# RWKV-7 state recurrence followed by a GELU MLP on one core: wide DRAM rows for the weights and for x, a planner with measured transfer times and one PSUM reader at a time, and MLP work spread over its chunk

## The chip, the cores and the metric

One core of one Trainium2 chip. The metric is the device time of one execution, in microseconds (us). The comparison of before and after rests on runs on the same chip.

## The reference

An attention-like recurrence for 4 batches, 8 heads, 768 steps and head dimension 40, and an MLP on its output:

```
for t in range(S):
    y[:, :, t] = einsum('bhd,bhde->bhe', rt, state)
    Sa = einsum('bhde,bhe->bhd', state, at)
    state = state * wt[:, :, None, :] - einsum('bhd,bhe->bhde', Sa, bt) + einsum('bhd,bhe->bhde', vt, kt)
x = y.transpose(0, 2, 1, 3).reshape(3072, 320)          # tokens x (heads * 40)
h = x @ w_in                                            # 320 -> 2048
out = (h / (1 + exp(-1.702 * h))) @ w_out               # 2048 -> 320
```

All inputs but the two weights are float32; the weights arrive as float64 and are taken as 64-bit integers.

## The kernel before

**Chunks and units.** The 768 steps are cut into 12 chunks `c` of 64 steps. A chunk has two units `i = 2c + p`, one for each pair of batches, so there are 24. In a unit the recurrence over 64 steps is solved as matrix work for 16 (batch, head) pairs: decays (`decay`: logarithm, running sums, exponentials), score matrices (`prep`: tiles `ps_NT`, `ps_A`, `ps_Av`, `ps_RV`), the triangular solve in six levels (`solve`: `ps_N`, then `ps_level`, each level in two halves, with the results `W` and `E` copied from PSUM by ScalarE and VectorE), then `ps_saT`, `ps_M` and the readout `ps_y`. The state goes from unit `i` to `i + 2` through `zraw`, `bz` and `zT`. All matmuls are float32 on 64x64 quarters of the array, four side by side; the profile has two records for each.

**From y to the MLP.** When `ps_y` of a unit is done, VectorE adds the state's part (`y`), GpSimd or VectorE multiplies by the decays (`x`, line 783), the SyncE queue (SP) writes `x` to DRAM (`part_with`, line 793, two DMAs, `x_dram`) and reads it back with channels on partitions (`get_back`, line 797, two DMAs, `xT`). When both units of a chunk are back, the MLP of that chunk may start.

**MLP.** `mlp(c)` has 40 `up` tasks (160 matmuls of 256 columns into `ps_up`), four GELUs on ScalarE (line 819, into `g`), and 2 x 8 `down` tasks (128 matmuls of 320 columns into `ps_down`), copies of the result to `ob` and its store.

**Weights.** `weight` brings a float64 tile of 512 columns, splits each number into sign and exponent and 52 bits of fraction on VectorE and ScalarE, joins them by matmuls with the identity (`ps_weight`), and scales the result into `w_in_sb` or `w_out_sb`. There are 10 tiles of each. A tile is used in the order of the first chunk's MLP.

**What sets the order.** Nothing is issued as written: every step is a task of `Plan` with a rank, the engines that can do it with an estimated duration on each, the tiles that it reads and writes, and a PSUM pair (two banks; there are four pairs). `Plan.order` walks through an estimated time: whenever an engine is free it takes the ready task of the lowest rank that it can do. Ranks are 10 for each unit and from 10000 up for the MLP, so that MLP tasks fill what the recurrence leaves free on TensorE. The result is the instruction order of each engine; on the chip each engine follows its own list in order and waits where a task isn't ready. All DMAs are on SP's queue. The planner also estimates when TensorE's code arrives, in blocks of 256 instructions (`FETCH`), and picks a task with longer matmuls where the code would run out (`AHEAD`). The estimates are in `Task` (`ns + 60.0` on VectorE and ScalarE), `DELAY` (from an engine's end to the next engine's start) and the line of `wire` (1500 ns and 280 bytes per ns for a DMA).

Of the kernel before, what the change touches and what calls it, by code (L numbers as in the profile page):

```python
# [49 lines left out]
class Task:  # L50
    def __init__(self, rank, engines, fn, pair, most, size):
        self.instr, self.sbuf = engines.pop("instr", 0), engines.pop("sbuf", False)
        self.rank, self.fn, self.pair, self.most, self.size = rank, fn, pair, most, size
        self.engines = {e: ns + 60.0 if e in ("DVE", "ACT") else 1.15 * ns if e == "POOL" else ns for e, ns in engines.items()}
        self.after, self.then = set(), []


class Plan:
# [5 lines left out]
    BLOCK, FETCH, AHEAD = 256, (3450.0, 4250.0, 5000.0), 300.0  # L64
    DELAY = {"PE": 330.0, "DVE": 130.0, "ACT": 130.0, "POOL": 150.0, "SP": 100.0}
    ISSUE = 60.0
# [28 lines left out]
    def order(self):  # L95
        for n, t in enumerate(self.tasks):
            t.n, t.left, t.ready = n, len(t.after), 0.0
            for o in t.after:
                o.then.append(t)
# [3 lines left out]
        coming = [(0.0, t.n) for t in self.tasks if not t.left]  # L103
        heapq.heapify(coming)
        able, now, wire, out, many = [], 0.0, 0.0, [], set()

# [11 lines left out]
        def fetch(at):  # L118
            return self.FETCH[(wire > at + 1000.0) + (wire > at + 10000.0)]
# [12 lines left out]
        def ahead(t):  # L132

            return (issued % self.BLOCK + t.instr) * fetch(now) / self.BLOCK - (now + t.engines["PE"] - begun)

        while coming or able:
# [12 lines left out]
            if not took:  # L149
                later = [x for x in (*free.values(), *pairs) if now < x < float("inf")]  # L150
# [17 lines left out]
            if t.pair is not None:  # L168
                if t.pair not in held:
# [9 lines left out]
            for o in t.then:  # L179
                o.ready = max(o.ready, end + (0.0 if o.engines.keys() == {e} else self.DELAY[e]))  # L180
                o.left -= 1
                if not o.left:
                    heapq.heappush(coming, (o.ready, o.n))
# [3 lines left out]
        return out  # L187


@with_exitstack  # L190
def rwkv7_gelu_quick(ctx: ExitStack, tc: tile.TileContext, time_d, v_d, w_d, wc_d, ak_d, b_d, rv_d, w_in, w_out, out):
# [6 lines left out]
    DFF = w_in.shape[1]  # L198
    NF = DFF // 128
# [4 lines left out]
    W_IN, W_OUT, PIECE = 2, 25, 512  # L204
# [113 lines left out]

    w_in_sb = single("w_in_sb", [128, NK, NM, 128])
# [6 lines left out]
    def weight(n, rank, key, dst, parts):  # L326

# [12 lines left out]

        def fetch(t):
# [40 lines left out]
        plan.add(rank, {"SP": 60.0 * len(parts)}, fetch, writes=T("wt"), size=128 * PIECE * 8, **here)  # L382
# [9 lines left out]
    def weights():  # L392
        blocks = w_in.rearrange("(k p) (m r f) -> k r p m f", p=64, r=2, f=128)
        for n, (m, k) in enumerate(product(range(0, NM, 4), range(NK))):
            weight(n, W_IN + 0.2 * n, ("w_in", (m // 4, k)), w_in_sb[:, k, m:m + 4].rearrange("p m f -> p (m f)"),
                   [(HALF[r], slice(0, PIECE), blocks[k, r][:, m:m + 4]) for r in BITS])
        for n in range(NF * DM // PIECE):
            parts, at = [], PIECE * n
            while at < PIECE * (n + 1):
                f, o = divmod(at, DM)  # L400
                size = min(DM - o, PIECE * (n + 1) - at)
                parts.append((slice(0, 128), slice(at - PIECE * n, at - PIECE * n + size), w_out[f * 128:(f + 1) * 128, o:o + size]))
                at += size
            weight(n + 10, W_OUT + 0.8 * n, ("w_out", n), w_out_sb[:, PIECE * n:PIECE * (n + 1)], parts)
# [10 lines left out]
    def load_w(i):  # L415
        for name, of, src, n in (("wc", wc_of, wc_d, 528), ("logw", logw_of, w_d, DM)):
            plan.add(10 * i - 30, {"SP": 60.0}, lambda t, of=of, src=src: nc.sync.dma_start(of(i), src[i]),
                     writes=[(name, i)], size=128 * n * 4)

    def load(i):  # L420
        for name, of, src, n in (("ak", ak_of, ak_d, 1024), ("time", time_of, time_d, 3 * DM), ("b", b_of, b_d, 512),
# [6 lines left out]
            plan.add(10 * i - 4, {"SP": 60.0 * len(rows)}, go, writes=[(name, i)] + ([("v", i)] if name == "RV" else []),  # L428
# [71 lines left out]
    xT_of = lambda c: buf("xT", c, [128, NK, 256])  # L500
# [4 lines left out]
    def prep(i):  # L505
# [12 lines left out]
        for n, (name, dst) in enumerate((("kh", kh_of), ("bh", bh_of))):  # L518
            plan.add(R + 4, {"POOL": 900.0, "DVE": 490.0, "sbuf": True}, lambda t, n=n, dst=dst: of(t.engine).tensor_mul(  # L519
# [56 lines left out]
    def solve(i):  # L576
# [207 lines left out]
        plan.add(R + 6, {"DVE": 1200.0, "POOL": 2000.0, "sbuf": True}, decayed, reads=T("y", "FT"), writes=T("x"))  # L784


        rows = lambda: drams[i].rearrange("(j e d) n -> e d j n", e=2, d=D)

        def part_with(t):
            if i not in drams:  # L790
                drams[i] = dram.tile([DM, 2 * C], FP32, tag=f"x{i}", name="x_dram")
            for e in BITS:
                nc.sync.dma_start(rows()[e], x_of()[64 * e:64 * e + D].rearrange("p j b t -> p j (b t)"))

        def get_back(t):
            for h in HALF:
                nc.sync.dma_start(xT_of(c)[h, :, 128 * p:128 * p + 128], drams[i].rearrange("(k q) n -> q k n", q=64))
        plan.add(-50, {"SP": 120.0}, part_with, reads=T("x"), writes=T("xd"), size=DM * 512)
        plan.add(-50, {"SP": 120.0}, get_back, reads=T("xd"), writes=[("xT", c), ("xs", (c, p))], size=2 * DM * 512)
# [6 lines left out]
    def mlp(c):  # L806
        R = 10000 + 100 * c

        def up(q, m, k):
            def go(t):  # L810
                ph, x = psum(t, "ps_up"), xT_of(c)[:, k]
# [11 lines left out]
        def down(p):  # L823
# [23 lines left out]
            plan.add(-100, {"SP": 120.0}, store, reads=[("ob", serial), ("out", serial)], size=128 * DM * 4)  # L847
# [28 lines left out]
    tasks = plan.order()  # L876
# [72 lines left out]
```

## Time and profile before

| | before |
|---|---|
| times of three runs, us | 878.48, 886.21, 884.02 (median 884.02) |
| the profiled execution's own time, us | 885.12 |
| its span, first to last instruction, us | 883.1 |
| busy in it, us: TensorE matmul, weight load, VectorE, ScalarE, GpSimd | 806.9, 629.5, 460.7, 382.3, 138.7 |
| mean granted TensorE clock | 0.979 |
| DMA: packets, MB, share of 16 engines | 58523, 82.61, 30.4% for the kernel's own queue |

The span runs from the first to the last instruction; about 2 us of the execution lie around it. Matmul and weight load overlap, and four matmuls run side by side, so the busy time of a group of matmuls is the time in which at least one of them ran. A busy TensorE can still be slowed: in the records matmuls have modelled ends.

### The profile page before, as it was taken

The page shows a single profiled execution, that of the slowest core. Times are in us where ns is not written, and L with a number is a line of the kernel's source. Part 1 is how long each engine was busy: PE and PEld are TensorE (multiplying, and loading weights), DVE is VectorE, ACT ScalarE, POOL GpSimd, SP SyncE. Part 2 cuts the span into 40 slices and gives each one's busy share as a digit, 9 for nine tenths or more (in the row PEclk, how much of TensorE's full clock was granted, in tenths as well). Part 3 has the DMA queues.
Part 4 walks back from the last instruction along what each step waited for, and adds up shares of the span by engine and source line. Part 5 has one row for each costly group of instructions (what it writes and reads, how often), then busy time and mean ns, then how long its engine had stood idle before and what let it go on. Part 6 is the DMA issues. An engine that isn't in the chain of part 4 may idle for free.

```text
span 883.1 us, 51576 instructions
## 1 busy us (share of the span) xinstructions
PE 806.9 (91%) x24272; PEld 629.5 (71%) x24272; DVE 460.7 (52%) x796; ACT 382.3 (43%) x678; POOL 138.7 (16%) x203
## 2 busy tenths in 40 slices
PE   3778899999989989889989989999979979999997
PEld 2445667888888877777777767877767767688764
DVE  6676873546545556445545554544555445354300
ACT  5547655335447346345444254533344333532210
POOL 2202130202202112202202102211021031010000
PEclk9989999999999999999999999999989989999999
DMA  9866551313322323322314232313142041020000
GB/s 265 252 172 184 170 148 41 119 40 109 112 81 75 110 71 88 105 75 87 104 40 125 89 92 75 115 41 112 49 129 82 21 126 56 23 75 26 19 25 16
DMA packets 58523, 82.61 MB, mean 94 GB/s; under 512 B 5672, under 2 KB 41512, under 8 KB 58312
## 3 DMA queue, kind: packets, MB, share of 16 engines
q1 hardware_dynamic: 58312, 79.32, 30.4%
q8 instruction: 190, 3.11, 1.5%
q14 instruction: 21, 0.17, 0.1%
HBM read 71.43 MB, written 7.86 MB: 90 GB/s over the span
## 4 chain that ended last, share of the span: by engine, by line
PE 77%; DMA 8%; ACT 6%; issue 4%; DVE 3%; SPq 2%; ACTq 0%
PE ps_up L236 23%; PE ps_down L236 21%; PE ps_level L236 15%; PE ps_weight L236 4%; PE ps_y L236 3%; DMA xT<-x_dram 3%; ACT W L698 3%; DMA x_dram<-x 3%; PE ps_N L236 2%; PE ps_M L236 1%; PE ps_Av L236 1%; PE ps_saT L236 1%; DVE E L693 1%; PE ps_rz L236 1%; PE ps_RV L236 1%
## 5 line engine op out<-in xcount | busy, mean ns | idle before, releaser
L236 PE MATMUL ps_up<-xT,w_in_sb 64*64 64x256 f32 x3840 | 277.6, 387 | 18.2 <-DMA xT<-x_dram 12.8
L236 PE MATMUL ps_down<-w_out_sb,g 64*64 64x320 f32 x3072 | 239.4, 431 | 0.7 <-issue 0.4
L236 PEld LDWEIGHTS ps_up<-xT,w_in_sb 64*64 64x64 f32 x3840 | 154.7, 137 | 53.9 <-issue 14.2
L698 ACT COPY W<-ps_level 128x672 f32<-128x672 f32 (+1 forms) x169 | 102.6, 617 | 191.7 <-PE ps_level L236 166.4
L236 PEld LDWEIGHTS ps_level<-W,E 64*64 64x64 f32 x5888 | 146.8, 137 | 41.9 <-DVE E L693 8.7
L236 PE MATMUL ps_level<-W,E 64*64 64x64 f32 (+2 forms) x5888 | 152.7, 235 | 8.9 <-DVE E L679 2.2
L236 PEld LDWEIGHTS ps_down<-w_out_sb,g 64*64 64x64 f32 x3072 | 122.1, 133 | 51.7 <-issue 2.2
L693 DVE TENSOR_TENSOR E<-twice,ps_level 128x512 f32<-128x512 f32 x120 | 81.5, 685 | 102.5 <-ACT W L698 75.6
L519 POOL TENSOR_TENSOR kh<-time,G 128x320 f32<-128x320 f32 x23 | 20.6, 897 | 503.1 <-issue 390.2
L236 PEld LDWEIGHTS ps_level<-W 64*64 64x64 f32 x2560 | 60.2, 133 | 23.6 <-issue 15.5
L819 ACT ACTIVATE g<-ps_up 128x1024 f32<-128x1024 f32 x48 | 49.2, 1024 | 62.7 <-PE ps_up L236 62.5
L236 PE MATMUL ps_level<-W 64*64 64x64 f32 (+2 forms) x2560 | 63.9, 234 | 9.4 <-issue 7.6
L236 PE MATMUL ps_weight<-wt,full 128*128 128x512 f32 x80 | 44.9, 692 | 6.6 <-ACT wt L369 3.4
L783 POOL TENSOR_TENSOR x<-y,FT 128x128 f32<-128x128 f32 x88 | 48.6, 582 | 0.5 <-ACT y L775 0.5
L677 DVE TENSOR_TENSOR W<-edge,ps_level 128x672 f32<-128x672 f32 x40 | 33.8, 848 | 19.1 <-PE ps_level L236 18.9
L511 POOL TENSOR_TENSOR ak<-ak,FT 128x512 f32<-128x512 f32 x21 | 27.5, 1309 | 55.3 <-ACT FT L474 33.6
L236 PE MATMUL ps_y<-RV,kh 64*64 64x104 f32 x768 | 36.1, 250 | 0.0
L236 PE MATMUL ps_y<-M,bh 64*64 64x104 f32 x768 | 35.7, 249 | 0.0
L843 ACT COPY ob<-ps_down 128x320 f32<-128x320 f32 x21 | 8.9, 425 | 60.8 <-PE ps_down L236 60.8
L845 DVE TENSOR_TENSOR ob<-ob,ps_down 128x320 f32<-128x320 f32 x24 | 11.6, 483 | 44.7 <-ACT ob L843 44.5
L236 PEld LDWEIGHTS ps_weight<-wt,full 128*128 128x128 f32 x80 | 15.2, 208 | 25.3 <-issue 16.5
L763 DVE TENSOR_TENSOR zraw<-ps_y,bz 128x320 f32<-128x320 f32 x20 | 9.8, 491 | 43.7 <-PE ps_y L236 43.7
(110 smaller groups left out, 1054.1 us busy)
## 6 DMA issues: line engine op xcount, KB each, us to landing
time<-in_time SPq DMA_DIRECT2D x24, 480.0 KB
RV<-in_v SPq DMA_DIRECT2D x24, 416.0 KB
xT<-x_dram SPq DMA_DIRECT2D x48, 160.0 KB
ak<-in_ak SPq DMA_DIRECT2D x44, 160.0 KB
rv<-in_rv SPq DMA_DIRECT2D x44, 160.0 KB
wc<-in_wc SPq DMA_DIRECT2D x24, 264.0 KB
wt<-in_w_in SPq DMA_DIRECT2D x20, 256.0 KB
logw<-in_w SPq DMA_DIRECT2D x24, 160.0 KB
```

Of the source, the lines that this page charges most:

```text
L236: nc.tensor.matmul(o, lhsT, rhs, start=start, stop=True, skip_group_check=True)
L511: plan.add(R, {"DVE": 690.0, "POOL": 1270.0, "sbuf": True}, lambda t: of(t.engine).tensor_mul(ahT(), ahT(), FT_of(i)), reads=T("ak", "FT") ...
L519: plan.add(R + 4, {"POOL": 900.0, "DVE": 490.0, "sbuf": True}, lambda t, n=n, dst=dst: of(t.engine).tensor_mul(dst(i)[:, :, :D], by_head(t ...
L677: plan.add(key, dve(672), lambda t: nc.vector.tensor_sub(W_of(s + 1)[:, :, b], edge[:, :, b], item(t)[:, :, :, :168]), reads=T("edge"), wr ...
L693: plan.add(key, dve(512), lambda t: nc.vector.tensor_sub(E_of(es + 1)[:, :, b].rearrange("p h j (n t) -> p h (j n) t", n=2), wide(twice).t ...
L698: plan.add(key, any2(4 * (168 - lo)), lambda t: copy(t.engine)(W_of(s + 1)[:, :, b, :, lo:], item(t)[:, :, :, lo:168]), writes=keeps, pair ...
L763: nc.vector.tensor_add(new, got, bz_of(i)[:, :, 64:].rearrange("p (u j) d -> p u j d", u=2))
L783: of(t.engine).tensor_mul(x[:, b ^ u, b], y_of()[:, at], FT_of(i)[:, at])
L819: plan.add(-45, act(1024), lambda t: nc.scalar.activation(g_of(c * NQ + q).rearrange("p m r n -> p r m n"), psum(t, "").rearrange("p r (m ...
L843: plan.add(-45, any2(320), lambda t: copy(t.engine)(ob_of(serial), psum(t, "")[:, 0, :DM]), writes=[("ob", serial)], pair=("down", serial))
L845: plan.add(-45, dve(320), lambda t: nc.vector.tensor_add(ob_of(serial), ob_of(serial), psum(t, "")[:, 1, :DM]), reads=[("ob", serial)], wr ...
```

## The change

- **Weights** come from DRAM in tiles that are laid out before the launch: one DMA of 128 rows of 4096 bytes for each tile, where there were two DMAs with rows of 1024 bytes (`w_in`) or two and three with 512 to 2560 bytes (`w_out`).
- **x** goes to DRAM in rows of 2048 bytes and comes back in rows of 2560, where both were 512. The channels of x get another order for that; the rows of `w_in` are put in the same order.
- **Planner.** The 60 ns on VectorE and ScalarE tasks are gone and hand-over delays are shorter; DMA issue costs are larger (350 for one DMA, 700 for two, where it was 60 and 120), a DMA takes 1200 ns and then 400 bytes per ns divided by 1.3; the code fetch takes 3550 ns and more when DMAs run beside it. A task that reads a PSUM pair on VectorE isn't placed while ScalarE reads that pair in the plan, and the other way round (`unread`).
- **Spread MLP.** `paced` makes the plan four times. After each, every MLP matmul task of a chunk gets a time before which the planner may not take it (`release`): the tasks are spread in proportion to their TensorE time from the moment the chunk's first one was ready to the moment the next chunk's was, 5 us earlier. The plan with the earliest estimated end is kept. A release is not in the program: it only moves the task's place in the order.

```diff
-        self.engines = {e: ns + 60.0 if e in ("DVE", "ACT") else 1.15 * ns if e == "POOL" else ns for e, ns in engines.items()}
+        self.engines = engines
...
-    BLOCK, FETCH, AHEAD = 256, (3450.0, 4250.0, 5000.0), 300.0
-    DELAY = {"PE": 330.0, "DVE": 130.0, "ACT": 130.0, "POOL": 150.0, "SP": 100.0}
+    BLOCK, FETCH, BESIDE, AHEAD = 256, 3550.0, 0.4, 300.0
+    DELAY = {"PE": 300.0, "DVE": 60.0, "ACT": 60.0, "POOL": 150.0, "SP": 800.0}
+    LATENCY, RATE, SPREAD = 1200.0, 400.0, 1.3
...
+        def unread(t, e):
+            return max((x + 60.0 for o, x in last.get(t.pair, {}).items() if o != e), default=0.0) if t.pair is not None and e != "PE" else 0.0
...
-                    took = next((t for t in able if e in t.engines and fits(t)), None)
+                    took = next((t for t in able if e in t.engines and fits(t) and unread(t, e) <= now), None)
...
-                wire = max(wire, now + 1500.0) + t.size / 280.0
-                end = wire
+                wire = max(wire, end + self.LATENCY)
+                running.append((wire, wire + self.SPREAD * t.size / self.RATE))
+                end = wire = running[-1][1]
...
+    def paced(self, groups, rounds, window, share):
+        best = None
+        for n in range(rounds):
+            out = self.order()
+            end = max(t.start + t.engines[t.engine] for t in out)
+            if best is None or end < best[0]:
+                best = end, [(t, {**vars(t)}) for t in out]
+            for g, then in zip(groups, groups[1:]):
+                whole, done, begin = sum(t.engines["PE"] for t in g), 0.0, g[0].ready
+                for t in g:
+                    new = begin + share * (then[0].ready - begin) * done / whole - window
+                    t.release = new if n == 0 else 0.5 * (t.release + new)
+                    done += t.engines["PE"]
...
-            for p, cols, part in parts:
-                to = raw()[p, cols]
-                nc.sync.dma_start(to.rearrange("p (m f) -> p m f", m=part.shape[1]) if len(part.shape) > 2 else to, part)
...
-        plan.add(rank, {"SP": 60.0 * len(parts)}, fetch, writes=T("wt"), size=128 * PIECE * 8, **here)
+        plan.add(rank, {"SP": 350.0}, lambda t: nc.sync.dma_start(raw(), src), writes=T("wt"), size=128 * PIECE * 8, **here)
...
-    xT_of = lambda c: buf("xT", c, [128, NK, 256])
+    xT_of = lambda c: buf("xT", c, [128, 2, NK, 128])
...
-        rows = lambda: drams[i].rearrange("(j e d) n -> e d j n", e=2, d=D)
+        rows = lambda: drams[i].rearrange("(e d j) n -> e d (j n)", e=2, d=D)
...
-                nc.sync.dma_start(rows()[e], x_of()[64 * e:64 * e + D].rearrange("p j b t -> p j (b t)"))
+                nc.sync.dma_start(rows()[e], x_of()[64 * e:64 * e + D].rearrange("p j b t -> p (j b t)"))
...
-                nc.sync.dma_start(xT_of(c)[h, :, 128 * p:128 * p + 128], drams[i].rearrange("(k q) n -> q k n", q=64))
-        plan.add(-50, {"SP": 120.0}, part_with, reads=T("x"), writes=T("xd"), size=DM * 512)
+                nc.sync.dma_start(xT_of(c)[h, p].rearrange("q k n -> q (k n)"), drams[i].rearrange("(q k) n -> q (k n)", q=64))
+        plan.add(-50, {"SP": 700.0}, part_with, reads=T("x"), writes=T("xd"), size=DM * 512)
...
-    tasks = plan.order()
+    tasks = plan.paced(list(paces.values()), ROUNDS, WINDOW, SHARE)
```

**What it moves.** Instruction counts on TensorE stay as they are; the order changes throughout. Three places follow, with the row numbers left out (`x8` are eight matmuls that follow each other).

TensorE in the program before, from the end of unit 17's readout (`ps_y`), the last piece of chunk 8 that its MLP waits for; between these rows and the first `ps_up` of chunk 8 stand 18 more `ps_level` rows and no row of the MLP:

```order
L236 MATMUL ps_y<-RV,kh_108 64x104 x4
L236 MATMUL ps_y<-M,bh_110 64x104 x4
L236 MATMUL ps_N<-bz_123,ak_117 64x104 x16
L236 MATMUL ps_zT<-ident,bz_123 64x40 x16
L236 MATMUL ps_A<-ak_118 64x64 x16
L236 MATMUL ps_cum<-logw,incl 64x160 x4
L236 MATMUL ps_level<-W 64x104 x4
L236 MATMUL ps_level<-W 64x64 x4
```

The same place now; one more row of eight `ps_down` matmuls stands among the rows that follow before the first `ps_up` of chunk 8:

```order
L270 MATMUL ps_y<-RV,kh_108 64x104 x4
L270 MATMUL ps_y<-M,bh_110 64x104 x4
L270 MATMUL ps_down<-w_out_sb,g 64x320 x8
L270 MATMUL ps_N<-bz_123,ak_117 64x104 x16
L270 MATMUL ps_down<-w_out_sb,g 64x320 x8
L270 MATMUL ps_RV<-rv_121 64x64 x16
L270 MATMUL ps_cum<-logw,incl 64x160 x4
L270 MATMUL ps_down<-w_out_sb,g 64x320 x8
L270 MATMUL ps_level<-W 64x104 x4
L270 MATMUL ps_level<-W 64x64 x4
```

Here 32 matmuls of chunk 7's MLP moved from ahead of the readout to behind it. Over chunks 2 to 10 the `ps_up` and `ps_down` matmuls between a chunk's last `ps_y` and its first `ps_up` number 16, 40, 48, 16, 0, 56, 0, 8 and 32 in the program before (216 together), and 24, 16, 48, 40, 32, 32, 32, 56 and 40 now (320). For chunk 11 they are 80 and 96.

SP's queue around the write and the return of `x` of unit 17, before:

```order
L427 DMA ak_117<-in_ak 40x1024 x2
L417 DMA logw<-in_w 128x320
L793 DMA x_dram<-x 40x4x128 x2
L427 DMA b_120<-in_b 40x512 x2
L797 DMA xT<-x_dram 64x5x128 x2
L417 DMA wc<-in_wc 128x528
```

And now:

```order
L448 DMA b_120<-in_b 40x512 x2
L438 DMA logw<-in_w 128x320
L814 DMA x_dram<-x 40x512 x2
L818 DMA xT<-x_dram 64x640 x2
L438 DMA wc<-in_wc 128x528
L863 DMA out<-ob 64x320 x2
```

The load of `b` moved ahead of the write, and nothing stands between write and return. For units 3, 5, 7 and 13 the store of a result (`out`) stands between the two now; before it was so for units 5, 11 and 23.

SP's queue at the start of the program, the first weight tiles, before:

```order
L427 DMA RV<-in_v 128x832
L344 DMA wt<-in_w_in 64x4x128 x8
L427 DMA ak_118<-in_ak 128x1024
L427 DMA time<-in_time 128x960
L427 DMA b_120<-in_b 128x512
```

And now:

```order
L448 DMA RV<-in_v 128x832
L411 DMA wt<-in_w_in 128x512 x4
L448 DMA ak_118<-in_ak 128x1024
L448 DMA time<-in_time 128x960
L448 DMA b_120<-in_b 128x512
```

The place is the same; eight DMAs became four. Of ScalarE's table loads, which stand where GELU follows an exponential or a logarithm or the other way round, the program has 48 before and 40 now.

More of the change, by code (lines that the diff above doesn't have):

```diff
@@ L118, in fetch @@
         def fetch(at):
-            return self.FETCH[(wire > at + 1000.0) + (wire > at + 10000.0)]
+            took = self.FETCH
+            for _ in range(3):
+                beside = sum(max(0.0, min(y, at + took) - max(x, at)) for x, y in running[-8:])
+                took = self.FETCH + self.BESIDE / self.SPREAD * beside
+            return took
+        def unread(t, e):
+            return max((x + 60.0 for o, x in last.get(t.pair, {}).items() if o != e), default=0.0) if t.pair is not None and e != "PE" else 0.0
         def fetched(t, start):
```

69 lines of the change are left out of this document (38 added, 31 removed).

## The prediction

> **What bounds the kernel now.** I read the chain that ended last first, then stretches of the span, then the places where TensorE's share falls. The page, and the windows of the span (columns: stretch, its length, busy us of matmul, weight load, VectorE, ScalarE, GpSimd with their counts, granted clock, DMA share, GB/s):
>
> ```profile
> PE 77%; DMA 8%; ACT 6%; issue 4%; DVE 3%; SPq 2%; ACTq 0%
> 0.00:40.00 40.00, 19.48 (x616) 14.73 (x618) 26.93 (x54) 22.31 (x44) 11.64 (x27) 1.00 0.93 271
> 40.00:66.00 26.00, 21.57 (x341) 11.14 (x337) 18.69 (x34) 11.86 (x26) 1.44 (x2) 0.80 0.61 166
> 66.00:120.00 54.00, 47.63 (x1444) 32.50 (x1437) 40.28 (x71) 38.09 (x74) 12.01 (x16) 1.00 0.56 171
> 120.00:240.00 120.00, 118.71 (x3624) 98.08 (x3619) 64.81 (x109) 51.28 (x88) 21.09 (x30) 1.00 0.31 91
> 240.00:840.00 600.00, 561.07 (x17671) 449.04 (x17666) 308.53 (x526) 253.37 (x445) 92.48 (x128) 0.98 0.26 78
> 840.00:883.00 43.00, 38.43 (x636) 24.01 (x628) 1.46 (x3) 5.37 (x7) 0.00 (x0) 1.00 0.07 16
> ```
>
> TensorE holds the end: 77% of the chain are matmuls. It idles in two places: the start (40 - 19.5 and 26 - 21.6, together 25 us of the first 66) and the middle (600 - 561.1 = 39 us from 240 to 840, and a mean clock of 0.98 there, 12 us more). The rest is work that the change doesn't take away, since no matmul is removed.
>
> The middle's idle time has a place. I took, for chunks 2 to 11, the window from the end of the chunk's last `ps_y` to its first `ps_up`; the first, the seventh and the sum of the ten:
>
> ```profile
> 233.00:245.00 12.00, 9.38 (x364) 8.47 (x357) 9.38 (x16) 7.75 (x17) 6.75 (x9) 1.00 0.61 193
> 639.00:650.70 11.70, 6.61 (x294) 6.01 (x284) 8.57 (x14) 6.36 (x14) 6.47 (x9) 1.00 0.67 207
> sum 119.20, PE 93.63 PEld 78.25 DVE 83.38 ACT 52.88 POOL 53.56; mean PE 9.36 PEld 7.82 DVE 8.34 ACT 5.29 POOL 5.36
> ```
>
> 119.2 - 93.6 = 25.6 us of the 39 fall into 20% of the time: each chunk's x takes some 11 to 13 us from `ps_y` to `ps_up`, and TensorE has too little else to do. The chain in the seventh of them (start, us, what):
>
> ```profile
> 641.12 2.11 issue
> ...
> 644.82 2.62 DMA x_dram<-x
> ...
> 648.20 3.95 DMA xT<-x_dram
> ```
>
> The write and the return of x bound it, 6.6 us without what goes ahead. Behind them the granted clock falls; of six 20 us stretches from 240 on that show it, the first, the fifth and the last:
>
> ```profile
> 240.00:260.00 20.00, 17.69 (x609) 15.47 (x601) 10.96 (x20) 11.51 (x24) 2.93 (x3) 0.91 0.29 87
> 640.00:660.00 20.00, 13.87 (x410) 11.89 (x406) 11.82 (x20) 8.30 (x17) 6.14 (x9) 0.83 0.46 144
> 720.00:740.00 20.00, 17.40 (x536) 14.09 (x540) 7.43 (x15) 8.07 (x13) 0.12 (x1) 0.84 0.20 59
> ```
>
> **The change part by part.** All against the profiled execution's own 885.1 us (span 883.1), 1.1 us over the median of the runs shown.
>
> **1. MLP work behind the readout.** The unit prices of MLP matmuls, where they run alone at the end (two records for each matmul):
>
> ```profile
> 843.93 8.63 PE ps_up L236 x160
> 863.35 15.12 PE ps_down L236 x224
> ```
>
> 15.12 / 224 = 67.5 ns a record, 135 ns a `ps_down` matmul; 108 ns a `ps_up`. By the order, chunks 2 to 11 have 296 MLP matmuls in these windows before and 416 now. The 120 more are, at 135 ns, 16.2 us of work that depends on nothing there. It comes from places where TensorE runs without a gap (118.7 of 120 us from 120 to 240), so little is lost there. The bounds are 0 and the whole 25.6. I take **-15**: chunk 11 already had enough, chunk 3 gets less than before (16 for 40), but chunks 6, 8 and 9, the emptiest (0, 0, 8), get 32, 32 and 56, 4.3 us or more each. What is late next there is the level chain, whose steps wait for copies on ScalarE and VectorE.
>
> The SP queue is the other side of this part: between write and return of the odd units from 3 on nothing stands in six, a load in one (unit 15) and a store in four (3, 5, 7, 13). A store waits for a `ps_down` that the spread puts behind `ps_y`; it stands there where the plan has it ready before the write of x lands, so I cost it at nothing and keep it for the range.
>
> **2. The clock.** The lowered stretches follow chunks 2, 5, 6, 7, 8 and 9, with 16, 16, 0, 56, 0 and 8 MLP matmuls in the window; chunks 3, 4, 10 and 11, with 40, 48, 32 and 80, have none. So five of five windows with 16 or fewer lose it, and one of five with more. Now only chunk 3 has 16, and chunk 2 has 24. Two or three of seven such losses stay: 12 us become 4, **-8**, between 0 and -12.
>
> **3. Wide rows.** Rates where one kind of row prevails: 6 to 16 us (rows of 2 KB and up, later 1 KB), 30 to 36 (`w_in`, rows of 1 KB), 834 to 844 (x and a store, mostly 512 bytes):
>
> ```profile
> 6.00:16.00 10.00, 4.27 (x136) 4.04 (x136) 7.40 (x12) 4.94 (x13) 2.85 (x2) 1.00 1.03 325
> 30.00:36.00 6.00, 4.72 (x124) 3.01 (x124) 3.88 (x7) 2.49 (x5) 0.42 (x1) 1.00 1.00 267
> 834.00:844.00 10.00, 10.00 (x156) 5.69 (x152) 1.39 (x5) 0.43 (x2) 0.00 (x0) 1.00 0.25 67
> ```
>
> Per full share: 316, 267 and 268 GB/s. The sizes:
>
> ```profile
> wt<-in_w_in SPq DMA_DIRECT2D x20, 256.0 KB
> xT<-x_dram SPq DMA_DIRECT2D x48, 160.0 KB
> x_dram<-x SPq DMA_DIRECT2D x48, 80.0 KB
> ```
>
> `w_in`'s ten tiles are 5.2 MB, 19.6 us at 267 and 16.6 at 316: 3 us of a queue that is 0.93 busy in the first 40 us, ahead of the loads of unit 1. The chain of the start waits for these:
>
> ```profile
> 19.49 2.38 issue
> ...
> 44.15 3.31 DMA wt<-in_w_in
> ...
> 61.38 4.21 DMA wt<-in_w_in
> ```
>
> and, from the first row, for code that comes late while the queue is full. Three waits of 2 to 4 us, each shorter by a fifth, and 3 us less in front: **-5** for the start, between +2 (one large DMA where two small ones let others in) and -12 (half of the 25 us idle). For x, 0.49 MB a unit (two writes, two returns) at 316 for 268 is 0.28 us. Issuing the two returns costs less, too; one such row beside one of a load with a whole row for each partition:
>
> ```profile
> 17.83 0.33 SPq L427 DMA_DIRECT2D b<-in_b  x1
> 837.61 1.29 SPq L797 DMA_DIRECT2D xT<-x_dram  x2
> ```
>
> 1.29 becomes 0.66 or so: 0.9 us of 11, in the windows that still wait, which is inside the -15.
>
> The Trainium skill, "DMA: Bandwidth & Descriptors", section Specifications, gives 512 bytes as the least transfer for line rate. By it the x and `w_in` rows were wide enough, and the row part would bring 0 of the -5. The rates above speak against it by a sixth; I keep the rows.
>
> **4. Code.** TensorE's code comes in blocks:
>
> ```profile
> q8 instruction: 190, 3.11, 1.5%
> 620.00:640.00 20.00, 19.96 (x719) 15.21 (x710) 10.47 (x19) 6.24 (x14) 0.59 (x2) 1.00 0.19 51
> 540.41 1.18 PE ps_level L236 x64
> ```
>
> 3.11 MB in 190 blocks are 16 KB each. In the densest stretch 719 matmuls and as many weight loads went by in 20 us; at 256 instructions a block that is one in 3.56 us. A block of `ps_level` alone streams in 128 x 1.18 / 64 = 2.4 us, a block of `ps_down` in 8.6. So runs of small matmuls outrun their code, and the 4% "issue" of the chain (35 us, half of it at the start) is its price. I cut TensorE's order into blocks of 128 records and added each kind at its streaming price: 51 blocks were under 3.4 us, 36 are now; lifting every short block to 3.56 us costs some 7 us less than before. I take **-6**, between -10 (blocks at 4 us) and +5 (other blocks meet the loads now).
>
> The Trainium skill, "Runtime: NRT & Kernel Launch", section Instruction fetch mechanics, says that the fetch is hidden, because the sequencer dispatches slower than code arrives. By it this part is 0. The 2.1 and 2.4 us waits above that only "issue" ends speak against it.
>
> **5. ScalarE and VectorE.** 48 table loads become 40:
>
> ```profile
> L819 ACT ACT_TABLE_LOAD x20 | 25.7, 1283 | 1.7 <-PE ps_up L236 1.4
> ```
>
> 8 x 1.28 = 10.3 us of an engine that is 43% busy; perhaps a sixth lies on the chain: **-2**, between 0 and -10. Twenty `edge` pieces go from VectorE to ScalarE, 0.24 to 0.34 us each: **+1**. That a pair has one reader at a time adds no wait on the chip: there VectorE's `E` waits for ScalarE's `W` of the same pair already,
>
> ```profile
> L693 DVE TENSOR_TENSOR E<-twice,ps_level 128x512 f32<-128x512 f32 x120 | 81.5, 685 | 102.5 <-ACT W L698 75.6 <-PE ps_level L236 25.8
> ```
>
> 75.6 us in all, so the plan only learns of it.
>
> **Sum:** -15 - 8 - 5 - 6 - 2 + 1 = -35; 885.1 - 35 = **850 us**.
>
> **The rivals.**
>
> A, everything lands: parts 1 and 2 reach 25 and 12, the start 10, code 8, tables 4: -59, 826 us. For it: the windows are the whole pattern of the middle. Against: chunks 2 and 3 have 24 and 16 matmuls only.
>
> B, code takes over: where the gaps close, the same instructions have to come faster, and "issue" replaces the wait for x. Parts 1 and 2 bring half (-11), part 4 nothing, the rest stays (-6): 868. For it: waits for code stand in the windows too (641.12). Against: a block in 4.3 us was the mean from 120 to 840 (42590 instructions, 166 blocks), 3.56 is possible.
>
> C, the order isn't what the chip runs: gaps move to other places of the chunk, since the estimates fit no better; only the start and the tables come: 878.
>
> D, slower: the plan gave every VectorE and ScalarE step 130 ns of slack (60 on its time, 70 on the hand-over), which is gone. TensorE takes its list in order; where a `ps_level` stands too early, all behind it wait. There are 24 x 6 x 2 = 288 level groups. If each waits 0.13 us more, that is 37 us, and the gain is gone; the old slack on both copies of a step (0.26) would cost 75, 925 us. It decides from 0.12 us a group. I price it at 0.16: 46 us, 896. Against it, a hand-over as it runs:
>
> ```profile
> 29.18 0.73 ACT W L698
> 29.91 0.04 issue
> 29.95 0.96 PE ps_level L236 x40
> ```
>
> 0.04 us from copy to matmul: the shorter estimate of 60 ns is the nearer one.
>
> **How the numbers follow.** Forecast 0.52 (838 to 862), A 0.16, B 0.13, C 0.11, D 0.08. The range leaves out D and the lower part of A: **825 to 881**. A measurement of this kernel tells about 1% from no change. Under 875: forecast, A, nearly all of B, 0.79; within 1%: C and a little of B, 0.12; above: D and a mishap like it, 0.09.
>
> **What would show it.** Part 1: in the ten windows TensorE idles 10 us, not 25.6, with `ps_down` between the levels. Part 2: a clock of 0.99 or more, two or three dips in the middle. Part 3: 267 GB/s in the first weights become over 300, and the readout of unit 0 ends some 5 us ahead of 66. Part 4: "issue" 3% of the chain. Part 5: 40 table loads. Wrong it would be if idle time shows up at `ps_level` behind ScalarE or VectorE (D), or as long waits of the return of x behind a store.

## The result and the profile after

The changed kernel took 855.7 us (median of four runs, 842.8 to 865.8) where before took 885.1: a ratio of 0.9575 (95% interval 0.9493 to 0.9656). The ratio counts only runs within 1.5% of the fastest run of their kernel, here those of 842.8 and 849.6 us; the medians alone give 0.967. In a second measurement ("The changed kernel once more", below) it was 0.9655 (0.9597 to 0.9712). The forecast was 850. The profiled execution took 842.8 us, the fastest of its four, against 885.1 for that of before: -42.3 us to explain, some 13 more than the medians differ by.

The stretches of the changed kernel (the third stretch, 66 to 120 us, is left out; the last ends at 800 us, just ahead of the last chunk's MLP):

```profile
0.00:40.00 40.00, 26.58 (x696) 19.60 (x696) 31.29 (x60) 25.68 (x52) 14.09 (x30) 1.00 0.84 299
40.00:66.00 26.00, 17.55 (x356) 10.36 (x356) 19.28 (x36) 12.37 (x23) 4.92 (x6) 0.87 0.52 168
120.00:240.00 120.00, 116.46 (x3654) 97.25 (x3656) 64.26 (x102) 56.00 (x96) 22.62 (x32) 1.00 0.31 92
240.00:800.00 560.00, 540.80 (x17568) 459.22 (x17561) 309.92 (x524) 233.03 (x416) 94.64 (x130) 1.00 0.28 83
```

The middle idles 19.2 us in 560 where it idled 39 in 600, and its clock is 1.00 where it was 0.98. In the first 66 us TensorE is busy 7 us longer and then 4 us less: 26.6 us of the first 40 for 19.5, then 17.6 of 26 for 21.6. The windows from a chunk's last `ps_y` to its first `ps_up`, first, seventh and sum:

```profile
229.90:240.90 11.00, 9.33 (x345) 8.53 (x338) 10.01 (x16) 3.76 (x9) 6.44 (x9) 1.00 0.54 155
612.90:624.70 11.80, 10.38 (x362) 8.61 (x358) 9.90 (x17) 5.94 (x13) 6.46 (x9) 1.00 0.63 189
sum 116.90, PE 105.29 PEld 91.16 DVE 86.85 ACT 48.61 POOL 56.66; mean PE 10.53 PEld 9.12 DVE 8.69 ACT 4.86 POOL 5.67
```

They are as long as before (116.9 us for 119.2), so x comes back no sooner; they are fuller: 11.6 us idle for 25.6. TensorE's own list of waits has the return of x, before and after, as

```profile
PE ps_up L236 <- DMA xT<-x_dram: 12.8, 9, 3.3
```

```profile
PE ps_up L270 <- DMA xT<-x_dram: 4.4, 5, 1.5
```

(us in total, times, the longest).

How much of a stretch isn't work can be estimated from the trace: each matmul is priced at the spacing that its kind keeps where it runs without a gap at full clock (the streaming prices below), and the sum is taken from the length of the stretch. By that the time from the first `ps_up` of chunk 1 to that of chunk 11 has 43.9 us over the work in it, where it had 83.4. Of these 39.5 us, 14.0 are idle time of the windows, 13.6 are clock (27.2 us at half speed before, none now), and 12 are the rest, of which 5 are idle time between the windows and 7 aren't taken apart. The start, up to the first `ps_up`, has 39.7 us over its work for 43.8. Chunk 0's MLP, between the two, has 1.6 us more. The end (from chunk 11's first `ps_up`) has the same length, 39.3 and 39.4 us.

### The profile page after: what moved, and what is told of

Same layout as the page of the kernel before. It is cut to its first block, busy times and chain, and to the rows that moved or that the text cites. A ratio compares the mean times of both kernels' runs of the same rounds, so it can differ in the third digit from the quotient of the medians.

```text
span 841.1 us, 51510 instructions
## 1 busy us (share of the span) xinstructions
PE 787.0 (94%) x24272; PEld 653.6 (78%) x24272; DVE 470.3 (56%) x804; ACT 367.8 (44%) x657; POOL 143.6 (17%) x208
## 5 line engine op out<-in xcount | busy, mean ns | idle before, releaser
L270 PE MATMUL ps_up<-xT,w_in_sb 64*64 64x256 f32 x3840 | 268.1, 378 | 5.7 <-DMA xT<-x_dram 4.4
L270 PE MATMUL ps_down<-w_out_sb,g 64*64 64x320 f32 x3072 | 244.4, 431 | 1.8 <-DVE ob L866 1.5
L270 PEld LDWEIGHTS ps_up<-xT,w_in_sb 64*64 64x64 f32 x3840 | 158.2, 134 | 27.0 <-issue 4.0
L719 ACT COPY W<-ps_level 128x672 f32<-128x672 f32 (+1 forms) x157 | 97.5, 623 | 175.8 <-PE ps_level L270 164.9
L270 PEld LDWEIGHTS ps_down<-w_out_sb,g 64*64 64x64 f32 x3072 | 138.4, 133 | 36.4 <-issue 2.9
L270 PE MATMUL ps_level<-W,E 64*64 64x64 f32 (+2 forms) x5888 | 149.9, 230 | 8.0 <-issue 3.0
L270 PEld LDWEIGHTS ps_level<-W 64*64 64x64 f32 x2560 | 64.4, 137 | 17.1 <-issue 6.6
L866 DVE TENSOR_TENSOR ob<-ob,ps_down 128x320 f32<-128x320 f32 x24 | 11.6, 485 | 48.6 <-ACT ob L864 48.1
L761 DVE TENSOR_TENSOR M<-ps_M,upper 128x512 f32<-128x512 f32 x24 | 16.5, 690 | 38.3 <-PE ps_M L270 38.3
L719 DVE COPY W<-ps_level 128x672 f32<-128x672 f32 (+1 forms) x43 | 32.0, 745 | 9.2 <-PE ps_level L270 9.1
L646 ACT ACTIVATE edge<-W 64x160 f32<-64x160 f32 x64 | 21.4, 334 | 33.5 <-DVE W L625 32.9
```

The source lines that it names most:

```text
L270: nc.tensor.matmul(o, lhsT, rhs, start=start, stop=True, skip_group_check=True)
L646: nc.scalar.mul(dst, src, -1.0)
L719: plan.add(key, any2(4 * (168 - lo)), lambda t: copy(t.engine)(W_of(s + 1)[:, :, b, :, lo:], item(t)[:, :, :, lo:168]), writes=keeps, pair ...
L761: plan.add(R + 4, dve(512), lambda t: nc.vector.tensor_tensor(M_of(i)[:, :, :64].rearrange("p (e j) t -> p e j t", e=2), psum(t, "")[:, :, ...
L866: plan.add(-45, dve(320), lambda t: nc.vector.tensor_add(ob_of(serial), ob_of(serial), psum(t, "")[:, 1, :DM]), reads=[("ob", serial)], wr ...
```

## The experiments

All ratios are to runs of the kernel before on the same chip, with the 95% interval; the times in us are medians of all runs. Runs of one kernel differ by 3 to 25 us and a profile is of one of them, not always one near the median (876.2 us for rows alone, 856.9 without the spread), so small differences between profiles are used only where several agree. "Windows" are the ten windows of chunks 2 to 11, "the middle" is the time from the first `ps_up` of chunk 1 to that of chunk 11, and the waits of the weight load are the sums of the list of waits for that queue.

**Rows alone.** In the kernel before, the weights and x get the wide rows; the planner's numbers stay, and so does the order. A weight tile is now one DMA where it was two or three, so the run changes the width of the rows and the number of DMAs together.

```diff
-            for p, cols, part in parts:
-                to = raw()[p, cols]
-                nc.sync.dma_start(to.rearrange("p (m f) -> p m f", m=part.shape[1]) if len(part.shape) > 2 else to, part)
+            nc.sync.dma_start(raw(), src)
...
-        rows = lambda: drams[i].rearrange("(j e d) n -> e d j n", e=2, d=D)
+        rows = lambda: drams[i].rearrange("(e d j) n -> e d (j n)", e=2, d=D)
```

> The order of before on TensorE, VectorE, ScalarE and GpSimd, row for row, with the wide DRAM rows of the weights and of x. Theory S (the gain is the MLP work in the windows between a chunk's last readout and its first up matmuls, and the clock that it keeps): the windows have the same 296 MLP matmuls, each wait for x gets about 1 us shorter, the start 3 to 4 us: 875 to 882 us, idle time of the ten windows 18 to 22 us, the clock dips of the middle stay at four or more. Rival R (the wide rows bring most of it): 850 to 862, windows under 14 us idle, two dips or fewer.

0.9868 (0.9823 to 0.9914), 869.2 us: 6 us faster than the theory's range and 7 slower than the rival's. The place of the gain is the start, as the theory has it, but it is 7 us there for 3 to 4, and the windows don't idle less. Up to the first `ps_up`, before and with wide rows, and the sum of the windows with wide rows:

```profile
0.00:109.20 109.20, 77.88 (x2120) 51.87 (x2124) 78.17 (x146) 64.32 (x123) 22.09 (x42) 0.95 0.72 211
```

```profile
0.00:102.50 102.50, 79.17 (x2116) 54.48 (x2120) 75.65 (x146) 64.61 (x123) 22.51 (x42) 0.97 0.68 224
...
sum 118.60, PE 92.76 PEld 74.56 DVE 81.91 ACT 50.02 POOL 52.01; mean PE 9.28 PEld 7.46 DVE 8.19 ACT 5.00 POOL 5.20
```

The first `ps_up` comes at 102.5 us for 109.2. The windows idle 25.8 us for 25.6, and half speed in the middle is 31 us for 27. So the rows pay at the start. TensorE's waits for the return of x fall from 12.8 to 7.1 us in its list, but the windows are as long and as empty, so x's own rows pay nothing that shows in the time.

**The rows taken out of the changed kernel,** its order kept (`fetch` is that of the kernel before, two or three DMAs with narrow rows; x's rows are narrow again, too; the cut ends both lines early):

```diff
-        plan.add(rank, {"SP": 350.0}, lambda t: nc.sync.dma_start(raw(), src), writes=T("wt"), ...)
+        plan.add(rank, {"SP": 350.0}, fetch, writes=T("wt"), ...)
```

> The order of the changed kernel on TensorE, VectorE, ScalarE and GpSimd, row for row, with the narrow DRAM rows of before (weights in two or three DMAs a tile, x in rows of 512 bytes). Theory: the rows are worth what they were in the order of before, 6 to 9 us, nearly all of it before the first up matmul: 1 to 1.5% over the changed kernel, 855 to 865 us, the first up 4 to 8 us later, idle time of the ten windows within 4 us of 11.5. Rival (the rows were worth something in the windows, too, once those are nearly full): 865 to 875 us, windows 16 us or more.

0.9679 (0.956 to 0.9797), 851.6 us; the changed kernel's medians are 855.7 and 848.8, so the runs don't tell the two apart. First `ps_up` at 112.2 us (changed: 109.8, and 110.5 in its second profile), windows 12.5 us idle. In this order the rows are worth 2 us of the start and not 7: the theory's place, a third of its size.

At the first readout they are still worth 4.4 us (it begins at 59.0 us with wide rows, at 63.4 with narrow ones), where in the order of before they are worth 7.3 (57.1 for 64.4). The changed kernel's place ahead of it, with wide and with narrow rows (start, us, what, in brackets the idle time ahead and what ended it):

```profile
49.78 9.32 PE L270 MATMUL ps_weight<-wt,full 128*128 128x512 f32 x16 [6.38 <-ACT wt L395]
```

```profile
53.76 9.70 PE L270 MATMUL ps_weight<-wt,full 128*128 128x512 f32 x16 [4.94 <-ACT wt L400]
```

Eight matmuls of the weights (these alone use the whole array, 128*128 in the row) stand ahead of the first readout in one piece. TensorE waits for their fractions, 6.4 us with wide rows and 4.9 with narrow ones; then the first records run at half speed (five with wide rows, 0.85 us each where the later ones take 0.45). So 1.4 us of what the rows bring goes into a longer wait, and the lowered clock stays. In the order of before the wait ahead of the first of these matmuls gets shorter, narrow and wide rows:

```profile
53.17 2.90 PE L236 MATMUL ps_weight<-wt,full 128*128 128x512 f32 x4 [3.44 <-ACT wt L369]
```

```profile
48.20 2.15 PE L236 MATMUL ps_weight<-wt,full 128*128 128x512 f32 x4 [1.59 <-ACT wt L346]
```

That is 1.9 us, and the 16 records take 8.1 us for 10.5, since none of them runs at half speed any more. The 2 us that the changed order loses between the first readout and the first `ps_up` aren't explained.

**No spread:** the changed kernel with one plan.

```diff
-    ROUNDS, WINDOW, SHARE = 4, 5000.0, 1.0
+    ROUNDS, WINDOW, SHARE = 1, 5000.0, 1.0
```

> The changed kernel with one plan and no release times (ROUNDS = 1): wide rows, new estimates, one reader of a PSUM pair, no spread. Its windows have 272 MLP matmuls (chunks 2 to 11: 16, 24, 8, 40, 24, 16, 0, 32, 24, 88), 49 table loads. Theory S: the idle time of the windows and the dips come back, 870 to 882 us. Rival P (the measured estimates bring most of it, the spread little): 850 to 862 us. R: as P, 850 to 862.

0.9803 (0.969 to 0.9915), 868.5 us, the time of the rows alone and 1.5 us under the theory's range. The idle time is back:

```profile
sum 119.00, PE 94.12 PEld 78.78 DVE 92.34 ACT 49.88 POOL 55.80; mean PE 9.41 PEld 7.88 DVE 9.23 ACT 4.99 POOL 5.58
```

24.9 us, with 17 us at half speed in the middle. P and R asked for 850 to 862.

**The spread alone,** in the kernel before (`release` and `paced` added, rows and estimates as they were).

```diff
-    tasks = plan.order()
+    tasks = plan.paced(list(paces.values()), 4, 5000.0, 1.0)
```

> The kernel before, narrow rows and old estimates, with the spread alone (four plans, 5 us, share 1). Its windows have 584 MLP matmuls (32, 48, 48, 56, 64, 24, 64, 64, 80, 104) but 54 table loads where before has 48. Theory S: the windows idle 5 us or less and the middle's clock dips go: 848 to 862 us. P and R: little of the gain, 872 to 885.

0.9732 (0.9617 to 0.9847), 864.0 us, between the theory's range, which it misses by 2 us, and the rivals', which begins 8 us later.

```profile
sum 135.30, PE 124.62 PEld 97.38 DVE 91.05 ACT 52.71 POOL 52.88; mean PE 12.46 PEld 9.74 DVE 9.11 ACT 5.27 POOL 5.29
```

Windows 10.7 us idle, where the theory had 5 or less, and half speed in the middle 3.4 us for 27, as it had. Rows alone and spread alone add up to 4.0%, about the whole change (4.3 and 3.5% in its two measurements).

**The rule of one reader, taken out and put in alone.**

```diff
-            return max((x + 60.0 for o, x in last.get(t.pair, {}).items() if o != e), default=0.0) if t.pair is not None and e != "PE" else 0.0
+            return max((x + 60.0 for o, x in last.get(t.pair, {}).items() if o != e), default=0.0) if False else 0.0
```

The cut takes the rule out of the changed kernel; the other run adds the same function and its uses to the kernel before.

> The changed kernel without the planner's rule of one reader of a PSUM pair at a time; all else as in it. Its windows have 632 MLP matmuls, 54 table loads. On the chip VectorE waits for ScalarE's read of the same pair either way. Theory S: the windows are full, so the same as the changed kernel within 1%, 845 to 862. A rival U (the rule makes the plan fit the chip, and without it TensorE stands at steps whose copy comes about 0.7 us later than planned): 865 to 880, with idle time at ps_level in the middle 10 us over the changed kernel's.

> The kernel before with the planner's rule of one reader of a PSUM pair at a time alone: narrow rows, old estimates, no spread. 216 MLP matmuls in the ten windows, 55 table loads. Theory U (the rule by itself takes away waits of TensorE for ScalarE and VectorE, since the plan no longer puts TensorE at a step whose second copy comes late): 866 to 876 us, waits of the weight load for ScalarE and VectorE 35 to 42 us where before has 54. Rival E (the rule only mends the new, shorter estimates; the old ones had slack for it): 880 to 892, those waits 50 us or more.

Without the rule 0.9748 (0.9661 to 0.9836), 859.6 us: S's range by the median, but with U's sign in the trace. Windows 13 us idle, yet the middle idles 33 us for 21 with four half-speed stretches for none, and the weight load's waits for ScalarE and VectorE are 75 us for 38. Without the rule, then with it:

```profile
PEld ps_level L270 <- DVE E L714: 11.7, 23, 1.0
PEld ps_level L270 <- DVE E L709: 8.4, 19, 0.7
```

```profile
PEld ps_level L270 <- DVE E L709: 0.8, 1, 0.8
PEld ps_level L270 <- DVE E L714: 0.4, 2, 0.3
```

Alone in the kernel before the rule does nothing for the time: 1.0029 (0.9966 to 1.0092), 883.6 us, in E's range; those waits are 47 us for 54, between the two forecasts. So it mends the new, tighter estimates, as E had it; whether it is worth 1% in the changed kernel stays open, since the intervals overlap.

**The estimates of before,** with rows, spread and the rule; and **the old slack alone** in the changed kernel. The cut is the second; the first puts back the estimates of transfers, DMA issue and code as well.

```diff
-        self.engines = engines
+        self.engines = {e: ns + 60.0 if e in ("DVE", "ACT") else 1.15 * ns if e == "POOL" else ns for e, ns in engines.items()}
-    DELAY = {"PE": 300.0, "DVE": 60.0, "ACT": 60.0, "POOL": 150.0, "SP": 800.0}
+    DELAY = {"PE": 330.0, "DVE": 130.0, "ACT": 130.0, "POOL": 150.0, "SP": 800.0}
```

> Wide rows, the spread and the rule of one reader, with all estimates of before (60 ns, hand-over, code fetch, DMA). 636 MLP matmuls in the windows, 47 table loads. If the estimates bring nothing of their own (part costs as forecast): the same as the changed kernel within 1%, 848 to 862. If they bring what no other part explains: 866 to 876, with the waits for x small and waits for code or for ScalarE and VectorE 10 us larger.

> The changed kernel with the slack of before on VectorE, ScalarE and GpSimd (60 ns a task, 130 ns a hand-over for 60); transfers, code, rows, spread and the rule of one reader as changed. 448 MLP matmuls in the windows, 49 table loads. Rival D of the prediction (the slack kept TensorE from standing at steps that are not ready): 2% and more faster than the changed kernel, 825 to 840. If the shorter estimates fit the chip: 850 to 862, waits of the weight load for ScalarE and VectorE 45 us or more for 36 to 38.

0.9681 (0.9626 to 0.9736), 852.7 us, and 0.961 (0.9513 to 0.9708), 847.3 us. Both are the changed kernel's time. With the old slack the waits for ScalarE and VectorE fall to 30 us, where 45 or more was expected if the shorter estimates fit, but the windows idle 16 us (its profile is of the longest of its four runs, 855.5 us): a different order of the same worth.

With all old estimates the start is better and the middle worse: the first `ps_up` comes at 96.3 us, and the middle has 56 us over its work for 44 to 48. So the new estimates aren't without effect; what they cost and what they bring cancel. The first half shows in every profile with wide rows: first `ps_up` at 96.3 and 102.5 us where the order is that of the old estimates, at 105.6 to 116.2 where it is that of the new ones. Which of them does it is open. It is not the slack (116.2 us with the old one) and not the transfer time (109.4 with the old one, in the last experiment); the costs of a DMA issue and the code fetch weren't put back singly.

**The changed kernel once more,** unchanged.

> The changed kernel once more, to see what sets its spread from 842 to 866 us. If it is the clock: the runs at 0.985 have three to six half-speed stretches in the middle, each with a loss of 1.7 us, and the runs at 0.993 none; that explains 5 to 10 of the 20 us. If it is the transfers: the middle's excess over streaming differs by 10 us or more with the same clock.

0.9655 (0.9597 to 0.9712), 848.8 us, 847.3 to 854.4. Windows 11.5 us idle, 3.4 us at half speed in the middle, 47.5 us over the work for 43.9. The longest of the four runs has the lowest clock (854.4 us at 0.987), but 849.4 us has the highest (0.991) and 847.3 has 0.989, so neither expectation is shown. In the first measurement 842.8 and 849.6 us had 0.993, 861.8 and 865.8 had 0.987 and 0.985; 0.007 of 855 is 6 us, so the clock can be a part of those 23 us and not the whole. What the rest is stays open.

**Work held back by hand.** In the kernel before, the last four `down` tasks of a chunk wait in the plan for the next chunk's second readout.

```diff
+                if p == 1 and m >= NM - 4:
+                    late.setdefault(c, []).append(plan.tasks[-1])
...
+        if p == 1:
+            for t in late.get(c - 1, []):
+                t.after.add(plan.tasks[-1])
```

> The kernel before, its rows, estimates and planner, with one thing changed: the last four down tasks of each chunk (32 matmuls, 4.3 us) may not be placed ahead of the next chunk's second readout. So each of the windows of chunks 2 to 10 has 32 MLP matmuls (40 for chunk 5), in place of 16, 40, 48, 16, 0, 56, 0, 8 and 32; chunk 11 keeps 80; 51 table loads for 48. Theory S (work in the windows takes the idle time away, and the clock stays up behind it): idle time of the ten windows 9 to 14 us for 25.5, the half-speed stretches of the middle 7 us or less for 27, 854 to 866 us. Rival (the work is missed where it was taken from): the same windows, but idle time elsewhere in the middle grows from 15 us to 25 or more, 870 to 884.

1.0 (0.9943 to 1.0057): no gain (the medians of all runs are 892.5 us for 883.5), a miss for the theory as I had put it.

```profile
sum 114.50, PE 91.90 PEld 75.30 DVE 80.93 ACT 50.12 POOL 55.96; mean PE 9.19 PEld 7.53 DVE 8.09 ACT 5.01 POOL 5.60
```

The windows have 376 MLP matmuls for 296, and still idle 22.6 us. At the streaming prices they hold 50.6 us of MLP for 39.9, but 36.7 us of other matmuls for 42.2: the planner took recurrence work ahead of the readout where the MLP work had been. So 87 us of work in 117 where before has 82 and the changed kernel 100. The rest of the middle idles 21 us for 15, where the rival had 25 or more. The count of MLP matmuls wasn't the measure; all the work in the window is. The same for some of the other profiles, each window from the start of the last `ps_y` record, work at the streaming prices:

| kernel | length of the ten windows less the work in them, us | idle, us |
|---|---|---|
| rows alone | 39 | 25.8 |
| no spread | 37 | 24.9 |
| before | 35 | 25.6 |
| held back | 30 | 22.6 |
| changed | 19 | 11.6 |
| spread alone | 16 | 10.7 |
| spread 5 us later (next) | 11 | 6.4 |
| the same with the old transfer estimate | 8 | 5.1 |

The windows aren't the whole time. With all old estimates they idle 7.3 us and yet the kernel is no faster than the changed one (852.7 us), since the middle idles 20 us outside them, where the changed kernel idles 9.5. With the spread alone that is 23 us, without the rule of one reader 20, in the kernel before 15.

**A better version.** The spread 5 us later, and then also the transfer estimate of before.

```diff
-    ROUNDS, WINDOW, SHARE = 4, 5000.0, 1.0
+    ROUNDS, WINDOW, SHARE = 4, 0.0, 1.0
...
-                wire = max(wire, end + self.LATENCY)
-                running.append((wire, wire + self.SPREAD * t.size / self.RATE))
+                wire = max(wire, now + 1500.0)
+                running.append((wire, wire + t.size / 280.0))
```

> The changed kernel with the spread 5 us later (window 0 for 5000): 632 MLP matmuls in the windows for 416, 53 table loads for 40. Theory S: idle time of the windows 5 us or less for 11.5: 838 to 852 if the windows are worth filling further. Rival: the work comes from places that need it, and the tables cost: 852 to 866.

> The changed kernel with the spread 5 us later (window 0) and the transfer estimate of before (1500 ns and 280 bytes per ns); it places the readout of unit 0 ahead of eight weight matmuls that stood before it. 656 MLP matmuls in the windows, 51 table loads. If the measured transfer times help the middle: 850 to 860, as the later spread without them loses its gain. If they do not, and the first readout no longer waits for weights: 832 to 843, the first readout at 50 to 55 us for 60.

0.9579 (0.9525 to 0.9633), 843.8 us, in the theory's range and beside the changed kernel's 0.9655 on the same chip; and 0.946 (0.9396 to 0.9525), 831.8 us, 830.6 to 833.5 in four runs: the fastest kernel here.

```profile
240.00:790.00 550.00, 533.69 (x17468) 455.15 (x17462) 314.13 (x525) 245.86 (x418) 95.18 (x132) 1.00 0.27 83
...
sum 141.40, PE 136.30 PEld 112.59 DVE 100.59 ACT 57.11 POOL 56.45; mean PE 13.63 PEld 11.26 DVE 10.06 ACT 5.71 POOL 5.64
```

Its first readout ends at 45.7 us for 60.7, ahead of the eight matmuls of the weights, but the first `ps_up` still comes at 109.4: the start isn't what gains, against that part of the expectation. The middle has 36.0 us over its work for 43.9. That the "measured" transfer estimate is the better one for the plan isn't borne out; that the old one is better is likely and not shown, since the intervals of the two versions touch (0.9525) and they ran on different chips.

## Why the prediction was right, and where its terms were off

**Part 1, -15:** 14.0 measured, for the wrong reason in part. The price, 120 MLP matmuls at 135 ns, came out because the other work in the windows stayed (42 us, then 44). Held back by hand, 80 more MLP matmuls displaced half their time in other work and brought 3 us. The step that doesn't hold by itself is "It comes from places where TensorE runs without a gap, so little is lost there": the planner moves other work the other way, and gaps open elsewhere (the middle outside the windows idles 21 us held back by hand, 23 with the spread alone, 15 before). In the changed kernel it holds: the middle outside the windows idles 9.5 us, less than before, which the prediction had no term for. For the windows the spread is needed (no spread: 24.9 us idle) and enough (alone: 10.7).

**Part 2, -8:** 13.6, the term that was most too small. I kept a loss for windows with few MLP matmuls (chunks 2 and 3, with 24 and 16); they idle 1.7 and 1.9 us now and lose nothing. Idle time is the better sign, not the count. Over the 140 windows of fourteen profiles, a half-speed stretch began in or right behind 25 of 31 with 2.6 us idle or more, 9 of 34 with 1.5 to 2.6, and 1 of 75 with less; by the count it was 18 of 24 with 16 MLP matmuls or fewer, 17 of 80 with 17 to 60, and none of 36 with more. The end of the seventh window and what follows it, which ran at 0.83 before, now at full clock:

```profile
620.00:640.00 20.00, 17.42 (x639) 16.71 (x642) 12.25 (x22) 9.80 (x20) 2.69 (x3) 1.00 0.28 81
```

The Trainium skill, "TensorE: Matmul & The Clock Gate", section Part 1, has the clock halved after an idle window of about 3.4 us. The half-speed records here last 3.4 us or a multiple, which agrees. But no gap of 3.4 us is needed in this kernel: in the 3.4 us straight ahead of the first stretch at each of those 35 windows TensorE idled 1.3 to 3.0 us in the trace, in one piece or several.

**Part 3, -5:** about 4 (43.8 to 39.7, and 40.4 in the second profile), as a sum of +7 for the rows in the order of before and -3 for the new order, whose wait at `ps_weight` the prediction did not have. The readout of unit 0 ends 5 us earlier, as forecast (60.7 us for 66.0), but the first `ps_up` doesn't come earlier (109.8 for 109.2). The rates are clear: 6 to 16 us, with the weights in it, and the place where x comes back,

```profile
6.00:16.00 10.00, 4.46 (x136) 4.09 (x136) 8.50 (x17) 5.23 (x14) 2.85 (x2) 1.00 1.01 389
790.00:801.00 11.00, 11.00 (x171) 9.87 (x167) 1.28 (x5) 0.43 (x1) 0.00 (x0) 1.00 0.22 63
```

385 GB/s per full share for 316, and 286 for 268 in the stretch with x. The saving of 0.9 us on x's path is not there: the windows are as long with rows alone (118.6) as before (119.2). Its place in the sum was inside part 1 and cost nothing. By the 512 bytes that the Trainium skill, "DMA: Bandwidth & Descriptors", section Specifications, gives for line rate, the rows would have brought nothing; the rates above and 0.9868 with the same order speak against it, though no run has the wide rows without the smaller number of DMAs.

**Part 4, -6:** the sign agrees, the size isn't measured by itself. The weight load's waits that only "issue" ends are 69 us before, 61 with rows alone, 47 and 54 in the two profiles of the changed kernel; part of that is the start. The two largest rows, before and after:

```profile
PEld ps_level L236 <- issue: 20.2, 27, 2.6
PEld ps_weight L236 <- issue: 16.5, 47, 2.4
```

```profile
PEld ps_weight L270 <- issue: 20.8, 49, 6.3
PEld ps_level L270 <- issue: 12.0, 18, 1.3
```

The 6.3 us are the wait for the fractions shown above, which TensorE's list puts to ScalarE. That others are waits for code is borne out by the profile of before: of its 18 that last 1 us or more, 12 end 1.3 to 1.7 us after a block of code has landed. The sign "issue 3% of the chain" can't be read, since the chain of the changed kernel's page reaches back over a quarter of the span only.

**Part 5, -2 and +1:** 40 table loads, as counted, but no sign that they matter: the two fastest kernels have 53 and 51, the kernel before 48. One of the changed kernel's groups:

```profile
L840 ACT ACT_TABLE_LOAD x15 | 19.2, 1283 | 0.3
```

"The plan only learns of it" held for the rule of one reader in the kernel before (1.0029). With the new estimates it isn't nothing: 37 us of waits, most of which don't show in the time.

**The rivals.** A (826) was not reached by the changed kernel, but it is about where the better version is (831.8), by its road: the windows filled. B did not come: the waits that "issue" ends fell while the gaps closed. C is refuted by the windows and by the idle time outside them. D, slower by the lost slack, is refuted directly: with the slack put back the time is the same (847.3).

**The sum.** Against the profile, -35 is 7 us short of -42: clock 5.6 us more than forecast, other waits of the middle 5 more, start and tables 3 less. That the median of 855.7 lies 6 us on the other side of 850 is the spread of the changed kernel's runs (842.8 to 865.8); so the near hit is in part luck, and the two main terms, the windows and the clock, are what was right.

## What to carry to other kernels

When one engine waits for a round trip, lay all its work that falls between the request and the answer beside the length of that trip; filling it with one kind of work helps only if the scheduler doesn't take another kind out. Price the clock with the gap: here half of the gain of a fuller gap was the half speed behind it. And try a planner's estimates on the chip one by one: the spread and, in the order of before, the rows made this change; the finer estimates lost at the start about what they gained in the middle, and with the later spread one of them did better undone.

## What the runs showed that I had not expected

A long row is worth more than I took: 385 GB/s per full share with rows of 4 KB among the loads against 267 with rows of 1 KB, yet its gain at the start shrinks from 7 to 2 us in an order that waits 6.4 us for decoded weights ahead of the first readout. And 15 us of earlier first readout (45.7 for 60.7 us) did not bring the first MLP matmul forward at all.
